# Fetching the V rows of sampled blocks: plain DMAs with register addresses in place of indirect DMAs

## The chip, the cores and the metric

The kernel runs on one core of a Trainium2 chip. A core has a matrix engine (PE), three engines for elementwise work (DVE, ACT and POOL), and SP, whose queue here does nothing but issue DMAs. Each engine runs its own instruction stream in order and waits on semaphores for the others. The metric is device time in microseconds of one execution of the program; lower is better.

## The reference

Block-sparse attention, whose output feeds a feed-forward network with a softplus between its two products. Cut to what is computed:

```python
# q, k, v: (B=4, H=8, S=768, D=64); 24 blocks of 32 rows; sampled_blocks: (24, 3), shared by batches and heads
scores = q @ k.transpose / sqrt(D)
mask = |block_i - block_j| <= 1              # window
mask |= block_i or block_j is 0 or 23        # global rows and columns
mask[block qb, block kb] = True for kb in sampled_blocks[qb]
attn = softmax(where(mask, scores, -1e9))
x = (attn @ v) as (B*S = 3072, H*D = 512)
h = x @ w_in                                 # 512 -> 2048
g = max(h, 0) + log1p(exp(-|h|))
out = g @ w_out                              # 2048 -> 512
```

For most blocks of queries the keys and values that matter are eight blocks of 32: three of the window, blocks 0 and 23, and three sampled ones. Which blocks are sampled is known only at run time.

## The kernel before

**Units of attention.** The blocks of query rows are taken in 24 groups: 4 batches with 6 groups of four blocks (the last group of a batch has two). They stand in `order`. For each batch one more set is added (`whole`), for the rows of blocks 0 and 23, which attend to everything: 28 sets in `sets`. A set is worked in two units of two head pairs each. For a unit, `scores` multiplies queries (tile qc) with gathered keys (tile kg) on PE (L834 for a full group), DVE adds the mask and takes the maximum (L840), `exponents` runs on ACT (L890), `transposes` turns the probabilities on PE (L903) with copies by ACT and DVE (L908, L910), and `values` multiplies them with V rows (tile vg) on PE (L946: 32 instructions in a unit of a full group). `normalise` and `turn` (L975, L989) make the rows of x from that. `pieces` interleaves these: the scores run two units ahead of the values.

**Values in SBUF.** Two buffers, `vbuf[0]` and `vbuf[1]`, serve the sets in turn. In half 0 of a buffer stand the three window blocks of each of the four query blocks (96 partitions); in half 1 stand the three sampled blocks of each (96 partitions); the last 32 partitions of both halves hold blocks 0 and 23. `load_values(m + 2)` is called when the values of set m are issued, and its DMAs wait until PE has read the buffer. For a full group the window rows are one DMA of SP (L755, 96x4x512). The rows of blocks 0 and 23 stay in the buffer for a whole batch. They are loaded with a batch's first two groups (L767), for sets 0 and 1 as 32x512 (L764), which ACT copies three times (`spread_ends`, L737). A whole set fills the buffer with all of the batch's V rows (L748).

**Sampled rows before.** They are fetched by POOL with an indirect DMA for each query block (L773, 96 rows of 2 KB, 88 in all). Its row addresses stand in the tile ix, which `make_index` computes at the start: POOL writes iotas (io, L559), DVE casts them, multiplies the block numbers by 32, adds (L593, three instructions) and adds the start of each batch (L598, four). One more indirect DMA (L564) loads, at the very start, the first rows of V into set 0's buffer, with its own iota (first, L561). The issues are put in the list `value_work`; `attend` takes one from it, and one from `key_work`, at each step (`gather`), and `values` takes what is left of its set first.

**Sampled keys.** These come by POOL's copies from kT, the keys of a batch in SBUF (L715). Their addresses come from registers: `pack_blocks` packs the three block numbers of a query block in 15 bits, two query blocks in a word of the tile pk. `registers` loads such a word into a register of an engine once (L656, TENSOR_LOAD), and shifts and masks take a number from it. The copies of set 0 are on DVE and ACT.

**The rest.** The FFN (L268 to L497) follows behind the attention, mixed into it from about 120 us on. The weights are brought from 64-bit floats by a chain of ACT (L166, L170), DVE (L176, L183, L189, L207) and POOL (L193), one tick for each step of the attention; each weight tile is loaded by SP ten ticks before its conversion begins (L159, tile raw).

**What sets the order.** SP runs in the order of the code. POOL and DVE do so for the startup pieces, and with ACT in the second phase of the FFN; elsewhere a scheduler orders PE, ACT, DVE and POOL by its own model, so that a change in what one instruction waits for can move others. The two places of SP in the loop: `load_values(m + 2)`, `load_queries` (tile qc, L649) and the weight loads (L159) follow each other. SP's DMAs use eight completion semaphores in turn.

Of the kernel before, what the change touches and what calls it, by code (L numbers as in the profile page):

```python
# [8 lines left out]
F32 = mybir.dt.float32  # L9
F32R = mybir.dt.float32r  # L10
I32 = mybir.dt.int32
# [46 lines left out]
def sparse_attention_ffn(  # L58
# [482 lines left out]
    io = ac.tile([NR * BLOCK, 1], I32, name="io")  # L541
    first = ac.tile([P, 1], I32, name="first")
    iof = ac.tile([NR * BLOCK, 1], F32, name="iof")
    ixf = ac.tile([NR * BLOCK, NB], F32, name="ixf")
    ix = ac.tile([NR * BLOCK, B, NB], I32, name="ix")
# [8 lines left out]
    for i in range(NI):  # L554
        nc.gpsimd.iota(
            iu[i * BLOCK : (i + 1) * BLOCK], pattern=[[NI, NG]], base=1 + i, channel_multiplier=0
        )
    for s in range(NR):
        nc.gpsimd.iota(io[s * BLOCK : (s + 1) * BLOCK], pattern=[[0, 1]], base=0, channel_multiplier=1)  # L559
    for rows in (slice(0, NR * BLOCK), slice(NR * BLOCK, P)):  # L560
        nc.gpsimd.iota(first[rows], pattern=[[0, 1]], base=0, channel_multiplier=1)  # L561
    vbuf = [ac.tile([P, 2, NI, DM], F32, name=f"vg{n}") for n in range(2)]

    nc.gpsimd.indirect_dma_start(  # L564
        out=vbuf[0][:, 0, 0, :], out_offset=None, in_=v,
        in_offset=bass.IndirectOffsetOnAxis(ap=first, axis=0),
    )
    nc.vector.memset(mask, 0.0)
    nc.vector.memset(rp, 0.0)

# [13 lines left out]
        )  # L584
        nc.vector.tensor_copy(out=pk, in_=pkf[:, 1 : NB - 1])

    def make_index():
        nc.vector.tensor_copy(out=iof, in_=io)
        nc.vector.tensor_copy(out=rf, in_=blk.rearrange("p (i s w) -> p i s w", s=NR, w=2)[:, :, :, 0])

        for s in range(NR):
            rows = slice(s * BLOCK, (s + 1) * BLOCK)
            nc.vector.tensor_scalar(  # L593
                out=ixf[rows], in0=rf[rows, :, s], scalar1=float(BLOCK), scalar2=iof[rows, 0:1],
                op0=ALU.mult, op1=ALU.add,
            )
        for b in range(B):
            nc.vector.tensor_scalar_add(out=ix[:, b], in0=ixf, scalar1=float(b * S))  # L598

    def make_mask():  # L600
        nc.vector.tensor_copy(out=iuf, in_=iu)
# [65 lines left out]
    def gathered(work, m):  # L667
        while work and work[0][0] <= m:
            work.pop(0)[1]()

    wanted = []

# [16 lines left out]
    def gather_keys(m):  # L689
        b, g = order[m]  # L690
        ni = NI if g < NG - 1 else 2
        kd = kg[m % 2]

        def of_block(i):

            eng = (nc.vector if i < 2 else nc.scalar) if m == 0 else nc.gpsimd
            copy = nc.scalar.copy if m == 0 and i >= 2 else eng.tensor_copy
            if i == 0:
                at = kT[b][:, 4 * g : 4 * g + NR, :]
                pattern = [list(x) for x in at.ap]  # L700
# [8 lines left out]
            (r,) = registers(eng, [2 * g + i // 2])  # L709
            for s in range(NR):  # L710
                x = nc.s_assert_within(
                    eng.snap((r >> (16 * (i % 2) + 5 * s)) & 31), 0, LAST,
                    skip_runtime_bounds_check_because="a sampled block is one of the key blocks",
                )
                copy(  # L715
                    out=kd[:, i, 1 + NR + s, :], in_=kT[b][:, bass.ds(x, 1), :].rearrange("p n f -> p (n f)")
                )
# [21 lines left out]
    def load_values(m):  # L739
# [4 lines left out]
        if whole:  # L744
# [6 lines left out]
            return  # L751
        ni = NI if g < NG - 1 else 2

        i0 = 1 if m == 0 else 0
        nc.sync.dma_start(  # L755
            out=vd[0 : 3 * BLOCK, 0, i0:ni], in_=overlapping(v, b * S + (4 * g + i0) * BLOCK, ni - i0, 3 * BLOCK)
        )
        if g < 2:

            for c, lo in enumerate((b * S, (b + 1) * S - BLOCK)):  # L760
                i1 = i0 if c == 0 else 0
                if m < SPREAD:
                    if i1 == 0:
                        nc.sync.dma_start(out=vd[3 * BLOCK : P, c, 0], in_=v[lo : lo + BLOCK])  # L764
                    spread.append((vd[3 * BLOCK : P, c, 0:1], vd[3 * BLOCK : P, c, 1:]))
                    continue
                nc.sync.dma_start(  # L767
                    out=vd[3 * BLOCK : P, c, i1:],
                    in_=v[lo : lo + BLOCK].unsqueeze(1).to_broadcast([BLOCK, NI - i1, DM]),
                )  # L770

        def of_block(i):
            nc.gpsimd.indirect_dma_start(  # L773
                out=vd[0 : 3 * BLOCK, 1, i, :],
                out_offset=None,
                in_=v,
                in_offset=bass.IndirectOffsetOnAxis(ap=ix[:, b, 4 * g + 1 + i : 4 * g + 2 + i], axis=0),
            )

        value_work.extend((m, lambda i=i: of_block(i)) for i in range(ni))  # L780


    def folded(g, whole):
# [7 lines left out]
    def scores(n):  # L791
# [4 lines left out]
        nmax = st["nmax"] = wk.tile([P, 2, 2], F32, tag="nmax", name=f"nmax{n}", bufs=4)  # L796
        st["pr"] = [wk.tile([P, S], F32, tag="pr", name=f"pr{n}_{r}", bufs=4) for r in range(2)]
        if not whole and g == NG - 1:
            gathered(key_work, place[b, g])
# [19 lines left out]
            st["rows"] = P  # L819
            st["chunks"] = 2  # L820
        elif not whole:
            gathered(key_work, place[b, g])
            kd = kg[place[b, g] % 2]
            ni = NI
            rows = slice(0, ni * BLOCK)
# [187 lines left out]
    def pieces(n):  # L1013
# [7 lines left out]
        def score_piece():  # L1021
# [3 lines left out]
            if s < len(units):  # L1025
                scores(s)
                if scored is not None:
                    load_keys(scored + 2)
                m, a = units[s]
                b, g, whole = sets[m]  # L1030
                if whole and a == NA - 1 and b + 1 < B:

                    gathered(key_work, place[b, g])
                    for n_ in range(4):
                        load_kT(b + 1, n_)
                    load_keys()
# [39 lines left out]
    for n in range(WARM):  # L1076
        nc.tensor.matmul(warm[:, n % 4], ident, ident, start=True, stop=True)
    with tc.manual_schedule(engines={mybir.EngineType.DVE}):
        make_index()
        pack_blocks()  # L1080
        make_mask()
        load_keys(0)
        gathered(key_work, 0)
# [157 lines left out]
```

## Time and profile before

| | |
|---|---|
| time, median of 3 runs | 805.5 us (804.5, 805.5, 806.07) |
| the profiled execution's own time | 807.66 us |
| its span (first to last instruction) | 805.6 us |
| mean granted clock of PE | 0.979 |
| busy PE / DVE / ACT / POOL | 95% / 74% / 70% / 49% |
| indirect DMAs of sampled rows on POOL | 88, 87.9 us |
| bytes moved by DMA | 132.27 MB, 17.57 MB of it in POOL's queue |

The 2.1 us between the span and the time of that execution lie before the first and behind the last instruction. A busy share is a mean over startup, attention with weights being converted, attention with FFN, and FFN alone; the prediction looks at these stages apart.

### The profile page before, as it was taken

The page shows a single profiled execution, that of the slowest core. Times are in us where ns is not written, and L with a number is a line of the kernel's source. Part 1 is how long each engine was busy: PE and PEld are TensorE (multiplying, and loading weights), DVE is VectorE, ACT ScalarE, POOL GpSimd, SP SyncE. Part 2 cuts the span into 40 slices and gives each one's busy share as a digit, 9 for nine tenths or more (in the row PEclk, how much of TensorE's full clock was granted, in tenths as well). Part 3 has the DMA queues.
Part 4 walks back from the last instruction along what each step waited for, and adds up shares of the span by engine and source line. Part 5 has one row for each costly group of instructions (what it writes and reads, how often), then busy time and mean ns, then how long its engine had stood idle before and what let it go on. Part 6 is the DMA issues. An engine that isn't in the chain of part 4 may idle for free.

```text
span 805.6 us, 21589 instructions
## 1 busy us (share of the span) xinstructions
PE 767.6 (95%) x8188; PEld 622.6 (77%) x8188; DVE 597.4 (74%) x1292; ACT 563.4 (70%) x1235; POOL 397.2 (49%) x617
## 2 busy tenths in 40 slices
PE   8688889999899999999999999999999999999997
PEld 8456657777677778777788878888998888988785
DVE  5667898887777777777655657888688797886654
ACT  4767877877687777777665767677776767766552
POOL 6663695543456426455100005425489597695400
PEclk9779998999999999999999999999999999999999
DMA  8669898678697786965714686221302315020021
GB/s 246 214 186 309 256 228 268 189 252 269 183 260 223 242 274 209 256 200 161 246 43 154 218 265 212 68 96 48 105 27 80 104 39 172 12 78 16 27 79 52
DMA packets 61175, 132.27 MB, mean 164 GB/s; under 512 B 5712, under 2 KB 18128, under 8 KB 60048
## 3 DMA queue, kind: packets, MB, share of 16 engines
q1 hardware_dynamic: 55072, 112.41, 44.6%
q0 software_dynamic: 5712, 17.57, 7.6%
q8 instruction: 64, 1.05, 0.6%
q10 hardware_dynamic: 288, 0.93, 0.3%
q14 instruction: 39, 0.32, 0.1%
HBM read 100.47 MB, written 30.41 MB: 162 GB/s over the span
## 4 chain that ended last, share of the span: by engine, by line
PE 55%; DVE 14%; ACT 14%; POOL 8%; issue 4%; DMA 2%; another core or an unknown queue 1%; POOLq 1%; SPq 0%; DVEq 0%; ACTq 0%
PE h L268 8%; PE h L269 7%; PE h L270 7%; PE o L495 5%; ACT pr L890 5%; PE o L496 5%; PE o L497 5%; PE t L903 3%; PE x L946 3%; POOL gq L337 3%; PE s L834 3%; DVE e L285 3%; POOL y L471 2%; PE acc L442 2%; PE acc L441 2%
## 5 line engine op out<-in xcount | busy, mean ns | idle before, releaser
L285 DVE SCALAR_TENSOR_TENSOR e<-u,e 128x512 f32<-128x512 f32 (+1 forms) x108 | 86.1, 797 | 94.4 <-ACT u L283 90.3
L337 POOL TENSOR_TENSOR gq<-gq 128x128 f32<-128x128 f32 x160 | 110.8, 715 | 63.1 <-DVE gq L322 60.0
L890 ACT ACTIVATE pr<-pr,nmax 128x256 f32<-128x256 f32 (+1 forms) x192 | 102.2, 534 | 33.1 <-DVE nmax L840 16.4
L773 POOL DMA_INDIRECT vg<-in_v_dram,ix x88 | 87.9, 998 | 69.8 <-PE x L946 38.3
L294 ACT ACTIVATE u<-u 128x512 f32<-128x512 f32 (+1 forms) x108 | 63.1, 584 | 71.7 <-DVE e L285 70.0
L715 POOL COPY kg<-kT 128x128 f32 x252 | 84.6, 380 | 52.0 <-PE s L834 43.2
L272 ACT ACTIVATE e<-h 128x512 f32<-128x512 f32 (+1 forms) x108 | 59.0, 547 | 57.5 <-PE h L270 57.1
L268 PE MATMUL h<-x,w 128*128 128x512 f32 x240 | 95.7, 399 | 2.4 <-ACT gh L275 1.0
L270 PE MATMUL h<-x,w 128*128 128x512 f32 x240 | 94.6, 394 | 0.0
L269 PE MATMUL h<-x,w 128*128 128x512 f32 x240 | 94.6, 394 | 0.0
L193 POOL TENSOR_TENSOR wt<-wt,raw 128x512 int32<-128x512 int32 x32 | 43.1, 1348 | 70.1 <-ACT raw L170 48.2
L283 ACT ACTIVATE u<-e 128x512 f32<-128x512 f32 (+1 forms) x108 | 63.1, 585 | 17.7 <-DVE gl L359 14.2
L840 DVE CUSTOM_DVE_ANT_1 pr<-s,mask 128x256 f32<-128x256 f32 x160 | 58.1, 417 | 23.3 <-PE s L834 10.4
L268 PE MATMUL h<-x,w1all 128*128 128x384 f32 x192 | 69.1, 360 | 3.4 <-DVE e L289 2.5
L903 PE MATMUL t<-ident,pr 128*128 128x128 f32 x448 | 65.6, 288 | 6.3 <-DVE x L1008 2.4
L270 PE MATMUL h<-x,w1all 128*128 128x384 f32 x192 | 65.2, 340 | 0.0
L269 PE MATMUL h<-x,w1all 128*128 128x384 f32 x192 | 65.2, 340 | 0.0
L277 ACT ACTIVATE e<-e 128x512 f32<-128x512 f32 (+1 forms) x108 | 63.0, 584 | 1.8
L903 PEld LDWEIGHTS t<-ident,pr 128*128 128x128 f32 x448 | 51.3, 145 | 14.1 <-issue 2.8
L946 PEld LDWEIGHTS x<-vg,pt 128*32 128x32 f32 x2560 | 42.8, 114 | 24.0 <-issue 22.4
L495 PE MATMUL o<-w1all,gh 128*128 128x512 f32 x144 | 61.3, 426 | 0.0
L946 PE MATMUL x<-vg,pt 128*32 128x64 f32 x2560 | 53.1, 228 | 7.6 <-issue 7.5
(141 smaller groups left out, 2049.4 us busy)
## 6 DMA issues: line engine op xcount, KB each, us to landing
vg<-in_v_dram SPq DMA_DIRECT2D x19, 768.0 KB
xD<-x SPq DMA_DIRECT2D x8, 1536.0 KB
raw<-in_w_in_dram SPq DMA_DIRECT2D x16, 512.0 KB
raw<-in_w_out_dram SPq DMA_DIRECT2D x16, 512.0 KB
qc<-in_q_dram SPq DMA_DIRECT2D x24, 256.0 KB
vg<-in_v_dram SPq DMA_DIRECT2D x12, 512.0 KB
yD<-os SPq DMA_DIRECT2D x24, 256.0 KB
x<-xD SPq DMA_DIRECT2D x4, 1536.0 KB
```

The source lines that it names most:

```text
L268: nc.tensor.matmul(ph, wh[:, cols], hi[:, c], start=(c == 0), stop=False)
L269: nc.tensor.matmul(ph, wh[:, cols], lo[:, c], start=False, stop=False)
L270: nc.tensor.matmul(ph, wl[:, cols], hi[:, c], start=False, stop=(c == NC - 1))
L283: nc.scalar.activation(u, e, AF.Copy, bias=1.0)
L285: nc.vector.scalar_tensor_tensor(out=e, in0=u, scalar=-1.0, in1=e, op0=ALU.add, op1=ALU.subtract)
L337: nc.gpsimd.tensor_tensor(out=a[:, to], in0=a[:, x], in1=a[:, y], op=op)
L495: nc.tensor.matmul(po[m], gh[:, cols], wh, start=first, stop=False)
L715: copy(out=kd[:, i, 1 + NR + s, :], in_=kT[b][:, bass.ds(x, 1), :].rearrange("p n f -> p (n f)"))
L773: nc.gpsimd.indirect_dma_start(out=vd[0 : 3 * BLOCK, 1, i, :], out_offset=None, in_=v, in_offset=bass.IndirectOffsetOnAxis(ap=ix[:, b, 4 * ...
L890: nc.scalar.activation(x, x, AF.Exp, bias=nmax[rows, r, j : j + 1], scale=-1.0, accum_out=rs[rows, h : h + 1])
L903: nc.tensor.transpose(ps[:, i, 0:rows], st["pr"][r][0:rows, c * P : (c + 1) * P], ident[0:rows, 0:rows])
L946: nc.tensor.matmul(xq[rows, h * D : (h + 1) * D], pt[r, 2 * j + c][:, rows], vd[:, c, i, h * D : (h + 1) * D], start=(c == 0), stop=(c == 1),)
```

## The change

The sampled rows of V are no longer fetched by POOL. `load_values` issues them on SP, directly behind the window rows: for each query block and each of its three sampled blocks one DMA of 32 rows of 512 numbers (64 KB), with the address from a register. There are 12 for a full group and 6 for the last of a batch, 264 in all. The register words are loaded by SP once, eleven in all. `make_index`, its tiles, the iotas and the indirect DMA of the first rows go; of `make_index` only the cast of the block numbers stays (`read_blocks`). Set 0 loads its window rows of all four blocks and the rows of both blocks 0 and 23 by plain DMAs. `value_work` is gone, so `gather` and `gathered` know the keys alone and `values` issues nothing first.

```diff
-    def make_index():
-        nc.vector.tensor_copy(out=iof, in_=io)
+    def read_blocks():
         nc.vector.tensor_copy(out=rf, in_=blk.rearrange("p (i s w) -> p i s w", s=NR, w=2)[:, :, :, 0])
-        for s in range(NR):
-            rows = slice(s * BLOCK, (s + 1) * BLOCK)
-            nc.vector.tensor_scalar(
-                out=ixf[rows], in0=rf[rows, :, s], scalar1=float(BLOCK), scalar2=iof[rows, 0:1],
-                op0=ALU.mult, op1=ALU.add,
-            )
-        for b in range(B):
-            nc.vector.tensor_scalar_add(out=ix[:, b], in0=ixf, scalar1=float(b * S))
...
-    key_work, value_work = [], []
+    key_work = []
     def gather():
-        for work in (value_work, key_work):
-            if work:
-                work.pop(0)[1]()
+        if key_work:
+            key_work.pop(0)[1]()
...
+    def sampled(eng, g, i, s):
+        (r,) = registers(eng, [2 * g + i // 2])
+        return nc.s_assert_within(
+            eng.snap((r >> (16 * (i % 2) + 5 * s)) & 31), 0, LAST,
+            skip_runtime_bounds_check_because="a sampled block is one of the key blocks",
+        )
...
-        i0 = 1 if m == 0 else 0
         nc.sync.dma_start(
-            out=vd[0 : 3 * BLOCK, 0, i0:ni], in_=overlapping(v, b * S + (4 * g + i0) * BLOCK, ni - i0, 3 * BLOCK)
+            out=vd[0 : 3 * BLOCK, 0, 0:ni], in_=overlapping(v, b * S + 4 * g * BLOCK, ni, 3 * BLOCK)
         )
...
-        def of_block(i):
-            nc.gpsimd.indirect_dma_start(
-                out=vd[0 : 3 * BLOCK, 1, i, :],
-                out_offset=None,
-                in_=v,
-                in_offset=bass.IndirectOffsetOnAxis(ap=ix[:, b, 4 * g + 1 + i : 4 * g + 2 + i], axis=0),
-            )
-        value_work.extend((m, lambda i=i: of_block(i)) for i in range(ni))
+        for i in range(ni):
+            for s in range(NR):
+                x = sampled(nc.sync, g, i, s)
+                nc.sync.dma_start(
+                    out=vd[s * BLOCK : (s + 1) * BLOCK, 1, i, :], in_=v[bass.ds(x * BLOCK + b * S, BLOCK)]
+                )
...
-        gathered(value_work, m)
         vd = vg[sets[m]]
...
-        make_index()
+        read_blocks()
         pack_blocks()
...
     with tc.manual_schedule(engines={mybir.EngineType.Pool}):
-        gathered(value_work, 0)
-        gathered(key_work, 1)
+        gathered(1)
```

In the changed kernel the lines of the scores are L808, of the values L919, of the key copies L695, of the window rows L734 and of the sampled rows L752.

Three places show what moves. First SP, at the loads of set 2 (the buffer that set 0 has left; vg is the buffer, qc_3 the queries of order place 3, raw the next weight tiles). Before:

```order
L755 DMA vg_174<-in_v_dram 96x4x512
L649 DMA qc_3_622<-in_q_dram 128x512
L159 DMA raw_662<-in_w_in_dram 128x512
L159 DMA raw_811<-in_w_out_dram 128x512
L755 DMA vg_175<-in_v_dram 96x4x512
```

and of the change the head of that stretch:

```order
L734 DMA vg_164<-in_v_dram 96x4x512
L633 TENSOR_LOAD pk
L633 ISA x2
L752 REGISTER_ALU
L752 ISA
L752 DMA vg_164<-in_v_dram 32x512
L752 REGISTER_ALU x2
L752 ISA
L752 DMA vg_164<-in_v_dram 32x512
```

and its end:

```order
L752 DMA vg_164<-in_v_dram 32x512
L626 DMA qc_3_686<-in_q_dram 128x512
L159 DMA raw_724<-in_w_in_dram 128x512
L159 DMA raw_871<-in_w_out_dram 128x512
L734 DMA vg_165<-in_v_dram 96x4x512
```

Between the window rows and the queries now stand twelve DMAs with their register steps, and a second TENSOR_LOAD after six of them; the queries, the weight tiles and the next set's window rows wait behind them.

Second POOL at the start, from its last iotas to the first key copy of set 1 (kg_180, later kg_169). Before:

```order
L561 IOTA first 96x1
L561 IOTA first 32x1
L564 DMA vg_174<-in_v_dram,first 128x512
L773 DMA vg_174<-in_v_dram,ix 96x512 x4
L656 TENSOR_LOAD pk
L656 ISA x2
L715 REGISTER_ALU
L715 ISA
L715 COPY kg_180<-kT_190 128x128
```

and now:

```order
L550 IOTA iu 32x6 x3
L633 TENSOR_LOAD pk
L633 ISA x2
L695 REGISTER_ALU
L695 ISA
L695 COPY kg_169<-kT_179 128x128
```

The five indirect DMAs ahead of the key copies are gone, and so are the iotas for them.

Third PE, where the scores of set 2 (s, from qc_2) and the values of set 1's first unit (x, from its V buffer) meet; y is the turning of set 0's rows, t the transposes of a unit. Before, the rows around the end of these scores:

```order
L834 MATMUL s_0_668<-kg_179,qc_2_418 32x256
L834 MATMUL s_1_669<-kg_179,qc_2_418 32x256
L989 MATMUL y_710<-ident,xs_640 128x128 x4
L946 MATMUL x_716<-vg_175,pt_0_645 32x64 x8
L946 MATMUL x_716<-vg_175,pt_4_652 32x64 x8
L946 MATMUL x_716<-vg_175,pt_0_645 32x64 x8
L946 MATMUL x_716<-vg_175,pt_4_652 32x64 x8
```

and now, from the transposes to the first of the scores:

```order
L877 MATMUL t_0_707<-ident,pr_0_485 128x128 x2
L877 MATMUL t_4_714<-ident,pr_1_486 128x128 x4
L919 MATMUL x_777<-vg_165,pt_0_708 32x64 x8
L919 MATMUL x_777<-vg_165,pt_4_715 32x64 x8
L919 MATMUL x_777<-vg_165,pt_0_708 32x64 x5
L808 MATMUL s_0_730<-kg_168,qc_2_456 32x256
L808 MATMUL s_1_731<-kg_168,qc_2_456 32x256
```

All 32 instructions of the values stood behind the scores; now 21 of them stand ahead and 11 behind. The following sets show the same with 21 to 25 of 32. The counts of instructions on PE and ACT are about the same as before.

More of the change, by code (lines that the diff above doesn't have):

```diff
@@ L540, in sparse_attention_ffn @@
     pk32 = pk.bitcast(I32)
[L541 to L545, printed above, removed]
     mask = ac.tile([P, NG, NS], F32, name="mask")
@@ L557, in sparse_attention_ffn @@
         )
-    for s in range(NR):
-        nc.gpsimd.iota(io[s * BLOCK : (s + 1) * BLOCK], pattern=[[0, 1]], base=0, channel_multiplier=1)
-    for rows in (slice(0, NR * BLOCK), slice(NR * BLOCK, P)):
-        nc.gpsimd.iota(first[rows], pattern=[[0, 1]], base=0, channel_multiplier=1)
     vbuf = [ac.tile([P, 2, NI, DM], F32, name=f"vg{n}") for n in range(2)]
-    nc.gpsimd.indirect_dma_start(
-        out=vbuf[0][:, 0, 0, :], out_offset=None, in_=v,
-        in_offset=bass.IndirectOffsetOnAxis(ap=first, axis=0),
-    )
     nc.vector.memset(mask, 0.0)
@@ L585, in pack_blocks @@
         nc.vector.tensor_copy(out=pk, in_=pkf[:, 1 : NB - 1])
-    def make_index():
-        nc.vector.tensor_copy(out=iof, in_=io)
+    def read_blocks():
         nc.vector.tensor_copy(out=rf, in_=blk.rearrange("p (i s w) -> p i s w", s=NR, w=2)[:, :, :, 0])
-        for s in range(NR):
-            rows = slice(s * BLOCK, (s + 1) * BLOCK)
-            nc.vector.tensor_scalar(
-                out=ixf[rows], in0=rf[rows, :, s], scalar1=float(BLOCK), scalar2=iof[rows, 0:1],
-                op0=ALU.mult, op1=ALU.add,
-            )
-        for b in range(B):
-            nc.vector.tensor_scalar_add(out=ix[:, b], in0=ixf, scalar1=float(b * S))
     def make_mask():
@@ L657, in registers, with gathered @@
         return [regs[eng, u] for u in us]
-    key_work, value_work = [], []
+    key_work = []
     def gather():
-        for work in (value_work, key_work):
-            if work:
-                work.pop(0)[1]()
-    def gathered(work, m):
-        while work and work[0][0] <= m:
-            work.pop(0)[1]()
+        if key_work:
+            key_work.pop(0)[1]()
+    def gathered(m):
+        while key_work and key_work[0][0] <= m:
+            key_work.pop(0)[1]()
+    def sampled(eng, g, i, s):
[4 more added lines that the diff above has]
+        )
     wanted = []
@@ L708, in of_block @@
                 end_keys(m, (first, nc.scalar.copy))
-            (r,) = registers(eng, [2 * g + i // 2])
+            registers(eng, [2 * g + i // 2])
             for s in range(NR):
[L711 to L714, printed above, removed]
+                x = sampled(eng, g, i, s)
                 copy(
@@ L760, in load_values @@
             for c, lo in enumerate((b * S, (b + 1) * S - BLOCK)):
-                i1 = i0 if c == 0 else 0
                 if m < SPREAD:
-                    if i1 == 0:
-                        nc.sync.dma_start(out=vd[3 * BLOCK : P, c, 0], in_=v[lo : lo + BLOCK])
+                    nc.sync.dma_start(out=vd[3 * BLOCK : P, c, 0], in_=v[lo : lo + BLOCK])
                     spread.append((vd[3 * BLOCK : P, c, 0:1], vd[3 * BLOCK : P, c, 1:]))
@@ L767, in load_values @@
                 nc.sync.dma_start(
-                    out=vd[3 * BLOCK : P, c, i1:],
-                    in_=v[lo : lo + BLOCK].unsqueeze(1).to_broadcast([BLOCK, NI - i1, DM]),
-                )
-        def of_block(i):
-            nc.gpsimd.indirect_dma_start(
-                out=vd[0 : 3 * BLOCK, 1, i, :],
-                out_offset=None,
-                in_=v,
-                in_offset=bass.IndirectOffsetOnAxis(ap=ix[:, b, 4 * g + 1 + i : 4 * g + 2 + i], axis=0),
-            )
-        value_work.extend((m, lambda i=i: of_block(i)) for i in range(ni))
+                    out=vd[3 * BLOCK : P, c],
+                    in_=v[lo : lo + BLOCK].unsqueeze(1).to_broadcast([BLOCK, NI, DM]),
+                )
+        for i in range(ni):
[4 more added lines that the diff above has]
+                )
     def folded(g, whole):
@@ L798, in scores @@
         if not whole and g == NG - 1:
-            gathered(key_work, place[b, g])
+            gathered(place[b, g])
             kd = kg[place[b, g] % 2]
@@ L821, in scores @@
         elif not whole:
-            gathered(key_work, place[b, g])
+            gathered(place[b, g])
             kd = kg[place[b, g] % 2]
@@ L1031, in score_piece @@
                 if whole and a == NA - 1 and b + 1 < B:
-                    gathered(key_work, place[b, g])
+                    gathered(place[b, g])
                     for n_ in range(4):
@@ L1082, in sparse_attention_ffn @@
         load_keys(0)
-        gathered(key_work, 0)
+        gathered(0)
     load_queries(1)
```

## The prediction

> **What bounds the kernel now.** I read the busy shares first, then the same shares by stage, because a mean over 800 us hides stages with different limits.
>
> ```profile
> PE 767.6 (95%) x8188; PEld 622.6 (77%) x8188; DVE 597.4 (74%) x1292; ACT 563.4 (70%) x1235; POOL 397.2 (49%) x617
> ...
> 0.00:120.00 120.00, 100.02 (x1610) 72.75 (x1614) 88.57 (x271) 85.18 (x214) 80.06 (x149) 0.91 0.82 240
> 120.00:425.00 305.00, 294.94 (x4493) 228.84 (x4493) 231.36 (x634) 226.49 (x584) 137.97 (x241) 0.98 0.72 217
> 425.00:806.00 381.00, 372.65 (x2095) 321.02 (x2093) 277.50 (x389) 251.72 (x437) 179.14 (x228) 1.00 0.29 98
> ...
> 100.00:120.00 20.00, 16.38 (x249) 11.76 (x247) 20.00 (x43) 16.13 (x43) 19.27 (x29) 1.00 0.90 228
> ```
>
> In the rows of windows the numbers after the length are the busy us of PE, PEld, DVE, ACT and POOL, then the granted clock, the DMA share and GB/s. From 120 us on PE is busy for 294.94 of 305 and 372.65 of 381 us: 18.4 us without a matmul in 686. The change takes no matmul away, so nothing much can be won there. In the first 120 us PE lacks 20 us. That is where this change can pay, and where it can hurt, since the DMA engines are 0.82 busy there. Around 100 to 120 us the bound is not PE: DVE has no idle time at all (20.00 of 20) and POOL hardly any (19.27).
>
> The waits of PE come next.
>
> ```profile
> PE x L946 <- issue: 7.5, 16, 1.1
> PE s L834 <- POOL kg L715: 3.2, 1, 3.2
> PE t L903 <- DVE x L1008: 2.4, 1, 2.4
> ```
>
> (Total us, times, longest.) No matmul of `values` (tile x, L946) waits for its V rows: its only wait is "issue". The indirect loads are in time today, so nothing is won by having sampled values sooner. What the change can win must come from POOL and DVE.
>
> **What leaves POOL.** The sampled loads are one group of the page:
>
> ```profile
> L773 POOL DMA_INDIRECT vg<-in_v_dram,ix x88 | 87.9, 998 | 69.8 <-PE x L946 38.3
> ```
>
> 88 issues of 998 ns, 87.9 us of POOL's 397.2. From 120 us on I take their value as nothing, because PE hides them: POOL is at 137.97 of 305 there. The largest thing that could be exposed behind POOL is the 2.4 us wait of L903 above; that is the upper end, and zero the lower. I take zero, since POOL is less than half busy.
>
> Before 120 us it differs. The rows of DVE and POOL around 115 us, with one L189 in a quiet place first:
>
> ```profile
> 34.39 0.74 DVE L189 SCALAR_TENSOR_TENSOR wt<-raw,wt 128x512 int32<-128x512 int32 x1
> ...
> 115.82 1.17 POOL L773 DMA_INDIRECT vg<-in_v_dram,ix  x1 [0.17 <-PE o L497]
> 117.01 1.29 POOL L193 TENSOR_TENSOR wt<-wt,raw 128x512 int32<-128x512 int32 x1
> 118.47 1.19 POOL L773 DMA_INDIRECT vg<-in_v_dram,ix  x1 [0.16 <-issue]
> 119.68 1.31 POOL L193 TENSOR_TENSOR wt<-wt,raw 128x512 int32<-128x512 int32 x1
> ...
> 116.57 2.30 DVE L189 SCALAR_TENSOR_TENSOR wt<-raw,wt 128x512 int32<-128x512 int32 x1
> 119.39 2.02 DVE L359 TENSOR_TENSOR gl<-u,gh 128x384 fp32r<-128x384 f32 x1
> 121.94 0.54 DVE L359 TENSOR_TENSOR gl<-u,gh 128x384 fp32r<-128x384 f32 x1
> ```
>
> L189 takes 0.74 us alone and 2.30 us here. It begins during the indirect, and ends 0.57 us after the L193 behind it. L359 does the same at 119.39: 2.02 us instead of 0.54, from inside the second indirect to after the second L193. I read this as DVE being held first by the indirect and then, POOL's next instruction being ready at once, by L193. Without the indirects both DVE instructions could finish in their usual time: (2.30 - 0.74) + (2.02 - 0.54) = 3.04 us. Both stand on the chain that ended last:
>
> ```profile
> 116.57 2.30 DVE wt L189
> ...
> 119.47 1.94 DVE gl L359
> ```
>
> So **3.0 us** is the gain that I can point to. Its lower end is nothing (L193 stays and can meet the same instructions elsewhere).
>
> The Trainium skill, "SBUF — State Buffer", section "Who interferes with whom", speaks against this gain. It says that a DVE instruction with two SBUF inputs collides with a GpSimd instruction that reads SBUF but not with one that only writes it, and infers that making DMA descriptors needs the write side alone. By that rule only L193 held these two and the 3.0 us stay, giving 805.5; the trace speaks rather against it, as L189 began 0.44 us before L193 and should have kept its place.
>
> **The start.** `make_index` loses eight DVE instructions (about 0.2 us each, ahead of the packing of the block numbers) and POOL eight indirects. The warm-up matmuls hide them:
>
> ```profile
> 1.45 14.35 PE L1077 MATMUL warm<-ident 128*128 128x128 f32 x100 [1.45 <-POOL ident masks.py:199]
> 15.73 2.18 PE L834 MATMUL s<-kg,qc 64*32 64x256 f32 x64
> ...
> 23.90 2.49 PE L834 MATMUL s<-kg,qc 64*32 64x256 f32 x32 [3.19 <-POOL kg L715]
> ...
> 12.43 4.38 POOL L715 COPY kg<-kT 128x128 f32 x12
> ```
>
> The first scores follow the warm-up directly. The scores of set 1 at 23.90 are put down to POOL's key copies, but these ended at 16.8, seven us earlier: they aren't what was late, and ending them sooner is worth nothing. I take 0, with 3.2 us (the whole idle time) as the other end.
>
> **What SP gets.** Twelve loads of 32 rows for each whole set, 264 in all. The same shape of DMA, the register loads, and the register steps as POOL does them for its key copies:
>
> ```profile
> L764 SPq DMA_DIRECT2D vg<-in_v_dram x3: 321/322/696, 2.7 to 10.4; - x3
> L656 POOLq TENSOR_LOAD <-pk x11: 5/286/502, 8.3 to 22.2; - x11
> 202.14 4.30 POOL L715 COPY kg<-kT 128x128 f32 x18
> ```
>
> (min/median/max ns.) One issue is 0.322 us; 18 copies with their register steps take 4.30 us, so the steps cost at most 0.239 us: 0.56 us a load, between 0.32 and, with the slowest issue in the rows below, 1.02. In all 264 x 0.56 = 148 us on a queue that now stands waiting for V buffers alone for 113.4:
>
> ```profile
> SPq L755 <- PE x L946: 113.4, 15, 13.5
> ...
> 33.05 0.34 SPq L755 DMA_DIRECT2D vg<-in_v_dram  x1
> 33.43 1.02 SPq L649 DMA_DIRECT2D qc<-in_q_dram  x1
> 34.49 0.43 SPq L159 DMA_DIRECT2D raw<-in_w_in_dram  x1
> 34.97 0.43 SPq L159 DMA_DIRECT2D raw<-in_w_out_dram  x1
> ...
> 36.14 0.99 PE L946 MATMUL x<-vg,pt 128*32 128x64 f32 x33
> 42.87 1.10 PE L946 MATMUL x<-vg,pt 128*32 128x64 f32 x64
> 47.68 0.87 PE L946 MATMUL x<-vg,pt 128*32 128x64 f32 x47
> ...
> 54.94 1.96 PE L834 MATMUL s<-kg,qc 64*32 64x256 f32 x32
> ...
> 23.29 1.47 SPq L159 DMA_DIRECT2D raw<-in_w_in_dram  x3
> ...
> 31.70 0.69 ACT L166 ACTIVATE wt<-raw 128x512 f32<-128x512 f32 x1
> 55.58 0.68 ACT L166 ACTIVATE wt<-raw 128x512 f32<-128x512 f32 x1
> ...
> 0.77 5.59 DMA blk<-in_blocks_dram
> ```
>
> Set 2 is the tight place. Its buffer comes free at 33.05 and its values are wanted at 47.68. A landing is taken as 5.59 us, the row of the block table. SP's DMAs take eight completion semaphores in turn, so an issue also waits for the landing of the one eight before it: 5.59 / 8 = 0.70 us a load, more than the 0.56. Twelve loads are issued by 33.05 + 0.34 + 12 x 0.70 = 41.8 and the last lands at **47.4**: just in time. Behind them on SP stand the queries of order place 3 and two weight loads, 8.4 us later than now. The queries move from 33.4 to 41.8 and are wanted at 54.94. The first of the two weight loads goes from 34.5 to 43 and is the fourth to be converted, at 55.58. So both are covered, by 7 us after the landing; without that cover up to 8.4 us would stand open, which the late rival holds.
>
> Sets 0 and 1 share one run of SP that begins when the block numbers are packed (8.3 us, the first register load). Set 0's twelve land at 8.3 + 0.3 + 8.4 + 5.6 = 22.6, and its values follow the scores of 23.90. Three window and end loads, another register load and set 1's twelve end at 17.0 + 0.3 + 15 x 0.70 = 27.8 and land at 33.4, wanted at 36.14. The first three weight loads follow at 28.2 instead of 23.29 and land by 34; the first conversion is at 31.70 now, but ACT's new order puts it behind the exponentials of the unit in front of it (2 us), so about 33.7. This too is just in time. Later sets have more room, as values take longer with FFN matmuls between them.
>
> **What PE gets.** The order of instructions on PE changes as well. At five places before about 86 us, 21 to 25 of the 32 instructions of `values` stand ahead of the next scores instead of behind them. All 32 are 64 matmuls of 1.10 us (42.87), so the scores start up to 25/32 x 1.10 = 0.86 us later, near 0.72 at the fewest; and the values are done as much earlier. I take nothing, because the sum of PE's work is the same; 5 x 0.72 = 3.6 us is the other end, and a gain of that size is as conceivable.
>
> **The sum.** The profiled execution took 807.66 us with a span of 805.6. 807.66 - 3.0 = 804.7; that execution is 2.2 us over the median 805.5, so the forecast is 805.5 - 3.0 = **802.5 us**.
>
> **Rivals.**
>
> **No change, 805.5 us.** The change does move the work, but PE hides all of it: DVE is held by L193 alone, or the weights that come sooner out of DVE wait for PE. For it: 95% PE. Against: L189 begins before L193.
>
> **Scores late, 809.1 us.** 3.6 us from PE's new order on 805.5. It decides if the start of scores ends the chain between 30 and 86 us, that is if ACT and DVE stand idle until those scores. For it: ACT's exponentials stand on the chain there, and PE waits in this stretch. Against: the values come earlier by the same amount. With the 3.0 us gained beside it the result would be 806.1, no change.
>
> **Sampled rows late, 813 us.** SP issues serially what POOL gathered in one piece. With 1.02 us a load, set 2 lands at 33.05 + 0.34 + 12.2 + 5.6 = 51.2, 3.5 us after 47.68. Three such sets (2, 3, 4, before FFN matmuls widen the gaps) give 10.6 us: 802.5 + 10.6 = 813. It decides at a landing above 5.7 us, which is 0.1 us from the row that I used; the DMA engines are 0.82 busy there. Against: that row is from the start, when all large loads are in flight.
>
> The Trainium skill, "DMA: Bandwidth & Descriptors", section "Rules for kernel authors", says to coalesce many small transfers and that under 64 KB one pays mostly overhead; these are 64 KB each. Its "Anatomy of one DMA" fits about 2.0 us + bytes / 436e3 (a fit for GpSimd's path), as an estimate 2.15 us each: 25.8 us for twelve in series, which would miss 47.68 by far, and 0.27 us each with eight in flight, which would not. No run here shows which.
>
> **How the numbers follow.** Forecast 0.40; no change 0.20; scores late 0.15; sampled rows late 0.25, as three places are in time by less than 3 us. The forecast's own range is 797 to 804: 802.5 less 3.2 (start) and 2.4 (L903) is 796.9, and half of the 3.0 lost is 804. The range of all reaches over no change and 809.1 to 813, and leaves out the worse half of the late rows. A measurement of this kernel can tell 0.2%, about 1.6 us: faster 0.40, within 0.20, slower 0.15 + 0.25 = 0.40.
>
> **What would show it.** Right: no L189 or L359 of 2 us between 100 and 125 us, DVE below 20.00 of 20 there, and no wait of L919 (the new line of values) for `vg`. Wrong: a wait of values for SP's loads in sets 0 to 4; a step of SP over 0.7 us a load; queries or weights that PE, ACT or DVE wait for; a start of scores that moved by more than 0.8 us with DVE idle before it. If DVE's holds are gone and the time is the same, the stretch was not on the path.

## The result and the profile after

The changed kernel takes **853.16 us** (median of 4 runs, 852.02 to 857.4) beside 805.67 us before: a ratio of 1.0602, 95% interval 1.0563 to 1.064. The forecast was 802.5 us, the range ended at 813: the sign was wrong.

The busy shares and the same three stages as before, the last one longer (columns: length, busy us of PE, PEld, DVE, ACT, POOL, clock, DMA share, GB/s):

```profile
PE 789.0 (93%) x8188; PEld 628.0 (74%) x8188; DVE 593.9 (70%) x1284; ACT 565.3 (66%) x1235; POOL 317.2 (37%) x523
...
0.00:120.00 120.00, 95.92 (x1552) 71.23 (x1553) 81.67 (x254) 80.36 (x201) 46.82 (x108) 0.90 0.74 215
120.00:425.00 305.00, 276.24 (x3910) 203.03 (x3911) 206.08 (x549) 202.05 (x519) 89.26 (x186) 0.98 0.72 207
425.00:851.00 426.00, 416.83 (x2728) 353.77 (x2727) 306.15 (x483) 282.92 (x516) 181.10 (x231) 1.00 0.30 102
```

POOL has lost its 80 us as planned. The span is 45.2 us longer (850.8 after 805.6 us), in two parts of about the same size. The time in which no matmul runs grows from 38.0 to 61.8 us. And PE's busy time grows too, from 767.6 to 789.0 us, for the same 8188 matmuls. (Busy is the time in which at least one matmul runs; matmuls overlap, and the profile models their ends.)

Between 120 and 425 us, where PE was busy for 294.94 of 305 us with 4493 matmuls, it is now busy for 276.24 with 3910. A stage in which "nothing can be won" had much to lose. The waits of PE (total, times, longest) name two new kinds:

```profile
PE o L495 <- ACT gh L347: 17.1, 13, 2.0
PE t L877 <- DVE nmax L814: 7.6, 13, 1.6
...
PE x L919 <- DMA vg<-in_v_dram: 3.7, 3, 2.3
```

PE stands at the projections of the FFN (tile o), waiting for ACT, and at the transposes, waiting for DVE. For the sampled rows themselves it waits only 3.7 us. SP's timeline around set 2 and the chain of waits there:

```profile
33.87 0.34 SPq L734 DMA_DIRECT2D vg<-in_v_dram  x1
35.13 13.34 SPq L752 DMA_DIRECT2D vg<-in_v_dram  x12
48.52 0.41 SPq L626 DMA_DIRECT2D qc<-in_q_dram  x1
...
33.87 11.13 DMA vg<-in_v_dram
...
48.52 2.83 DMA qc<-in_q_dram
51.49 1.96 PE s L808 x32
...
L752 SPq DMA_DIRECT2D vg<-in_v_dram x264: 315/316/1628, 8.5 to 463.8; - x132
...
DMA to landing us min/median/max: 1.7/3.5/11.7
```

An issue costs the 0.316 us that were expected, but twelve hold SP for 13.34 us, 1.11 us each. The window load ahead of them takes 11.13 us to land, the sampled loads queue behind it, and with eight of its DMAs in flight SP has to wait. Only then come the queries, at 48.52, and the scores start when they have landed.

PE's timeline at one later place shows the new order at work (the first row is the last of a run of eighteen projections that begins at 243.90):

```profile
247.95 0.39 PE L496 MATMUL o<-w1all,gh 128*128 128x512 f32 x1
248.27 0.32 PE L919 MATMUL x<-vg,pt 128*32 128x64 f32 x8
249.50 0.73 PE L497 MATMUL o<-w1all,gl 128*128 128x512 f32 x2 [0.91 <-DVE gl L359]
...
252.64 0.40 PE L497 MATMUL o<-w1all,gl 128*128 128x512 f32 x1
252.96 0.86 PE L919 MATMUL x<-vg,pt 128*32 128x64 f32 x42
253.75 1.09 PE L808 MATMUL s<-kg,qc 64*32 64x256 f32 x32
...
255.14 0.42 PE L919 MATMUL x<-vg,pt 128*32 128x64 f32 x14
```

Projections stand between a unit's values, and the next scores behind all of them. The 64 matmuls of the unit come in three pieces.

### The profile page after: what moved, and what is told of

Its sections match the earlier page's. It is cut to its first block, busy times and chain, and to the rows that moved or that the text cites. A ratio compares the mean times of both kernels' runs of the same rounds, so it can differ in the third digit from the quotient of the medians.

```text
span 850.8 us, 22839 instructions
## 1 busy us (share of the span) xinstructions
PE 789.0 (93%) x8188; PEld 628.0 (74%) x8188; DVE 593.9 (70%) x1284; ACT 565.3 (66%) x1235; POOL 317.2 (37%) x523
## 4 chain that ended last, share of the span: by engine, by line
PE 52%; DVE 15%; ACT 12%; DMA 8%; POOL 7%; issue 3%; SPq 2%; POOLq 0%; DVEq 0%; ACTq 0%
PE h L268 7%; PE h L270 7%; PE h L269 7%; DMA vg<-in_v_dram 5%; PE o L495 5%; PE o L497 5%; PE o L496 5%; ACT pr L864 3%; PE s L808 3%; POOL gq L337 3%; PE x L919 3%; DVE e L285 2%; POOL y L471 2%; DVE pr L814 2%; PE t L877 2%
## 5 line engine op out<-in xcount | busy, mean ns | idle before, releaser
L285 DVE SCALAR_TENSOR_TENSOR e<-u,e 128x512 f32<-128x512 f32 (+1 forms) x108 | 84.2, 780 | 89.8 <-ACT u L283 89.5
L695 POOL COPY kg<-kT 128x128 f32 x252 | 90.2, 404 | 131.4 <-PE s L808 111.4
L193 POOL TENSOR_TENSOR wt<-wt,raw 128x512 int32<-128x512 int32 x32 | 46.1, 1441 | 156.8 <-ACT raw L170 58.6
L919 PEld LDWEIGHTS x<-vg,pt 128*32 128x32 f32 x2560 | 47.6, 115 | 41.2 <-issue 26.8
L919 PE MATMUL x<-vg,pt 128*32 128x64 f32 x2560 | 64.2, 231 | 9.0 <-DMA vg<-in_v_dram 3.7
L497 PE MATMUL o<-w1all,gl 128*128 128x512 f32 x144 | 59.6, 422 | 3.8 <-DVE gl L359 3.8
```

The source lines that it names most:

```text
L285: nc.vector.scalar_tensor_tensor(out=e, in0=u, scalar=-1.0, in1=e, op0=ALU.add, op1=ALU.subtract)
L497: nc.tensor.matmul(po[m], gl[:, cols], wh, start=False, stop=last)
L695: copy(out=kd[:, i, 1 + NR + s, :], in_=kT[b][:, bass.ds(x, 1), :].rearrange("p n f -> p (n f)"))
L919: nc.tensor.matmul(xq[rows, h * D : (h + 1) * D], pt[r, 2 * j + c][:, rows], vd[:, c, i, h * D : (h + 1) * D], start=(c == 0), stop=(c == 1),)
```

## The experiments

Two theories: **SP**, that its queue holds back what stands behind the loads; and **PE's order**, that the scheduler's new order costs time by itself. To part them, PE is put in the order of the code. One line does it, and then the order on PE is the same whatever SP does:

```diff
-    with _tile.TileContext(nc) as tc, tc.manual_schedule(engines={_mybir.EngineType.SP}):
+    with _tile.TileContext(nc) as tc, tc.manual_schedule(engines={_mybir.EngineType.SP, _mybir.EngineType.PE}):
```

All ratios are to the kernel before, run on the same chip beside them (it took 804.6, 804.0, 793.4 and 793.3 us beside r1 to r4, r5 to r8, r9 to r12 and r13 to r15, so times of different groups aren't compared). Why the kernel before is 11 us faster in the last two groups isn't known; its granted clock is 0.979 to 0.988 in the first two and 0.987 to 0.995 in the last two. Ratios of the first two groups are therefore not compared with those of the last two to better than some 1.4%.

| run | ratio | 95% interval |
|---|---|---|
| the change | 1.0602 | 1.0563 to 1.064 |
| r1 before, PE in code order | 1.0068 | 1.0045 to 1.0091 |
| r2 the change, PE in code order | 1.0305 | 1.0261 to 1.035 |
| r3 r1 with dummy loads on SP | 1.0329 | 1.0274 to 1.0385 |
| r4 r2, one load a query block | 0.9884 | 0.9863 to 0.9906 |
| r5 r2, queries first | 1.0097 | 1.0064 to 1.013 |
| r6 r2, window behind | 1.0338 | 1.0267 to 1.0408 |
| r7 r2, loads spread | 1.0046 | 1.0017 to 1.0075 |
| r8 queries first, PE scheduled | 1.0817 | 1.0779 to 1.0855 |
| r9 r4 with free indirects | 1.0941 | 1.0909 to 1.0972 |
| r10 r4, PE scheduled | 0.9927 | 0.9896 to 0.9958 |
| r11 r7, PE in code order in the first phase | 1.0124 | 1.0093 to 1.0155 |
| r12 before, the same | 1.0033 | 1.0012 to 1.0055 |
| r13 r4 with gated indirects | 1.0577 | 1.0548 to 1.0606 |
| r14 r4 with gated copies on POOL | 1.0139 | 1.0112 to 1.0166 |
| r15 indirects in batch 0, then spread | 0.9963 | 0.9941 to 0.9985 |

**PE's order against SP: r1 to r4.**

r1 and r2 are the one line above on both kernels.

> The kernel before, with PE's instructions in the order of the code (nearly the order that it had). All theories: 803 to 809 us. It is the base for the other kernels with PE fixed.

> The changed kernel, with PE's instructions in the order of the code, so the same order on PE as in r1. PE's new order is the cause: 803 to 812 us. SP is the cause (twelve loads of 0.66 us and 4.7 us of waits for completion semaphores hold queries, weights and the next window back): 840 to 860 us, as the changed kernel itself (853). Both share it: between, 820 to 835.

r3, on r1:

```diff
+    dummy = [ac.tile([BLOCK, 16], F32, name=f"dummy{n}") for n in range(NR * NI)]
...
         value_work.extend((m, lambda i=i: of_block(i)) for i in range(ni))
+        if m >= SPREAD:
+            for i in range(NR * ni):
+                nc.sync.dma_start(out=dummy[i], in_=v[i * BLOCK : (i + 1) * BLOCK, 0:16])
```

> r1 with twelve loads of 32 x 64 bytes more on SP behind each window load from set 2 on (into a tile that nobody reads); the indirect DMAs stay on POOL. Time that SP is held is the cause: 825 to 850 us, since only queries, weights and next windows are later here. Sampled rows that land late, or their bytes, are the cause: 803 to 811.

r4, on r2:

```diff
         for i in range(ni):
-            for s in range(NR):
-                x = sampled(nc.sync, g, i, s)
-                nc.sync.dma_start(
-                    out=vd[s * BLOCK : (s + 1) * BLOCK, 1, i, :], in_=v[bass.ds(x * BLOCK + b * S, BLOCK)]
-                )
+            x = sampled(nc.sync, g, i, 0)
+            nc.sync.dma_start(out=vd[0 : 3 * BLOCK, 1, i, :], in_=v[bass.ds(x * BLOCK, 3 * BLOCK)])
```

> r2 with one load of 96 consecutive rows for each query block, from the first sampled number, in place of three of 32 (the other two sampled blocks and the batch's offset are left out). As many bytes, a third of the loads. Count on SP is the cause: 803 to 815 us. Bytes, or that values wait for SP's DMAs at all, is the cause: 840 to 860.

Both theories hold a share. From r2 to the change, with only PE's order set differently (ACT, DVE and POOL stay with the scheduler and follow it), the ratio goes from 1.0305 to 1.0602: some 24 us are PE's order. From r1 to r2, with PE's order the same, it goes from 1.0068 to 1.0305: some 19 us are SP, less what dropping the indirects gains. r3 loses as much by SP's time alone (1.0329), although the rows are still gathered by POOL and hardly a byte is added. r4 moves as many bytes in a third of the loads and is *faster* than before, and than the 803 to 815 us expected, so the bytes are not the matter. It leaves out two of the three sampled blocks and the batch's offset, and so do r9, r10, r13 and r14, which are built on it: they are probes and no kernels to use. Beside r4 (795.37 us), r2 (828.2 us) loses 33 us to its loads on SP.

The two shares look different on PE. The busy times of r1, then r2:

```profile
PE 762.3 (94%) x8188; PEld 617.1 (76%) x8188; DVE 597.6 (74%) x1292; ACT 563.7 (70%) x1235; POOL 396.1 (49%) x617
```

```profile
PE 764.3 (92%) x8188; PEld 623.5 (75%) x8188; DVE 591.3 (72%) x1284; ACT 564.9 (68%) x1235; POOL 309.9 (37%) x523
```

From r1 to r2 PE is busy about as long, and its time without a matmul grows from 45.3 us (of 807.6) to 62.0 (of 826.3): SP's share is waiting. From r2 to the change the time without a matmul stays, 62.0 and 61.8 us, and the busy time grows from 764.3 to 789.0: waits for queries give way to waits for ACT and DVE, and the share of PE's order is the same matmuls overlapping less. The granted clock isn't the reason, as it is higher in the change (0.978 after 0.968). The matmuls of the values show it, before and then in the change:

```profile
L946 PE MATMUL x<-vg,pt 128*32 128x64 f32 x2560 | 53.1, 228 | 7.6 <-issue 7.5
```

```profile
L919 PE MATMUL x<-vg,pt 128*32 128x64 f32 x2560 | 64.2, 231 | 9.0 <-DMA vg<-in_v_dram 3.7
```

One of them takes as long as before (231 and 228 ns), but together they are busy for 64.2 us instead of 53.1. A unit's 64 matmuls in one piece, here in r2, take 1.10 us; the three pieces above take 0.32 + 0.86 + 0.42 = 1.60.

```profile
149.68 1.10 PE L919 MATMUL x<-vg,pt 128*32 128x64 f32 x64
```

PE goes from the matmuls of one kind of tile (h, o, s, t, x, y, acc) to those of another 407 times in r2 and 486 times in the change.

What r2's PE waits for, first in its list:

```profile
PE s L808 <- DMA qc<-in_q_dram: 16.1, 7, 7.9
```

**What stands behind the loads: r5 to r8.** r5 (on r2) and r8 (on the changed kernel) issue the queries first:

```diff
                 values(n)
-                if ended[2] is not None:
-                    load_values(ended[2] + 2)
             if scored is not None:
                 load_queries(scored + 2)
+            if n < len(units) and ended[2] is not None:
+                load_values(ended[2] + 2)
```

> r2 with the queries issued on SP ahead of the next value loads instead of behind them. In r2 PE waits 16.1 us for queries (tile qc). Queries behind the loads are the whole cost of SP: 809 to 814 us. Weight loads, next windows or the sampled rows themselves are as late: 820 to 828.

> The changed kernel with the queries issued ahead of the next value loads, PE left to the scheduler. If the late queries are what made the scheduler collect FFN projections ahead of scores: 812 to 820 us. If its order stays bad for another reason: 835 to 853.

r6, on r2, issues the sampled loads ahead of the window load from set 2 on (`of_blocks` is the loop over i and s):

```diff
+        if m >= SPREAD:
+            of_blocks()
         nc.sync.dma_start(
             out=vd[0 : 3 * BLOCK, 0, 0:ni], in_=overlapping(v, b * S + 4 * g * BLOCK, ni, 3 * BLOCK)
         )
...
+        if m < SPREAD:
+            of_blocks()
```

> r2 with the window rows (and the rows of blocks 0 and 23) issued behind the twelve sampled loads from set 2 on. The waits for completion semaphores that window and weight loads hold (about 4.7 of 12.6 us a set) are a part of the cost: 815 to 823 us. Only the 0.66 us a load counts: 826 to 830, as the same twelve stand before the queries.

r7, on r2, puts the loads of a query block into the list `value_work` again, of which each step takes one entry:

```diff
-        for i in range(ni):
+        def of_block(i):
             for s in range(NR):
                 x = sampled(nc.sync, g, i, s)
...
+        value_work.extend((m, lambda i=i: of_block(i)) for i in range(ni))
```

> r2 with the twelve loads issued in portions of three, one portion at each step of the attention, as the indirect DMAs were, so that queries and weight loads aren't behind all twelve. What stands behind the burst is the cost: 796 to 806 us (POOL without indirects gave 795 in r4). The number of loads on SP is the cost, however they are placed: 820 to 828.

The queries are about half of what SP's loads cost r2 beside r4: r5 is at 1.0097, 2.1% or 17 us under r2, and PE's wait for them (16.1 us) is gone. It is still 2.1% over r4; its values now wait 6.9 us for V rows, and the rest isn't taken apart. r6 refutes a part of my account: with the window behind the sampled loads the ratio stays (1.0338) and PE still waits 16.3 us for queries:

```profile
PE s L814 <- DMA qc<-in_q_dram: 16.3, 5, 5.8
```

So the order of window and sampled loads doesn't matter while both stand ahead of the queries. r7 comes to 1.0046; its 807.53 us lie just over the 796 to 806 expected. And r8 lies outside both of its ranges: with queries first and PE left to the scheduler the kernel is slower than the change itself. From 120 to 425 us, r8 and then r5:

```profile
120.00:425.00 305.00, 275.79 (x3634) 196.38 (x3629) 199.25 (x544) 201.31 (x506) 86.15 (x189) 0.98 0.66 198
...
120.00:425.00 305.00, 292.75 (x4533) 227.21 (x4533) 226.89 (x636) 230.26 (x592) 85.57 (x187) 0.99 0.76 225
```

The same loads in the same order on SP, 3634 matmuls against 4533: here the order on PE, with what follows from it on ACT and DVE, costs 7%. Again most of it is busy time: 806.5 us after 764.5 in r5, with 588 changes from one kind of matmul to another after 407, while the time without a matmul grows from 49.3 to 58.8. Why the scheduler orders so was not tried; its model isn't in these runs.

**Where the gain of r4 comes from, and a kernel that keeps it: r9 to r15.** r10 is r4 with the scheduler's order on PE.

> r4 with PE left to the scheduler, which then gives the order of the kernel before: 786 to 795 us if the loss of the changed kernel is its loads on SP and the order that follows from them; over 800 if the scheduler's order costs time by itself.

At 0.9927 r10 is within its expectation: with few loads on SP, dropping the indirects gains 0.7% (0.4 to 1.0). The scheduler's order adds no busy time then (PE is busy 755.9 us, 755.4 in r4), though it isn't quite that of the kernel before. r4 gained 1.8% on r1. r1 and r4 between 40 and 70 us, and the waits that r1 has and r4 has not:

```profile
40.00:70.00 30.00, 24.32 (x542) 16.53 (x540) 22.02 (x71) 22.18 (x64) 19.62 (x31) 0.94 0.87 258
...
PE x L946 <- issue: 8.0, 14, 1.9
...
PE s L834 <- issue: 3.2, 5, 1.7
```

```profile
40.00:70.00 30.00, 27.36 (x556) 18.66 (x556) 26.97 (x83) 27.25 (x74) 11.26 (x23) 1.00 1.02 319
```

In r1 PE stops again and again inside one group of its matmuls, waiting for nothing that the profile shows, mostly while POOL issues indirects; DVE and ACT then have less to do. In r4 no wait of PE is put down to "issue". But the stalls don't follow from the indirects alone. r12, below, has all 88 of them and r1's order on PE, ACT, DVE and POOL up to the second phase of the FFN; it ran in the third group, and its only such wait is at the scores:

```profile
PE s L834 <- issue: 3.2, 3, 2.4
```

And r2 and r5, which have no indirects, have one stop of 2.1 us each at the values. What brings these stalls is open, and with it how much of r4's gain belongs to the indirects.

r9 and r13 were to put the issue of indirects back into r4 without their bytes, r14 POOL's time without a DMA. r9 (88 indirects of 96 rows of 64 bytes into tiles that nobody reads) and, behind the dots, the two lines that differ in r13 (80 indirects of 32 rows of 64 bytes into the last rows of the V buffer, which they overwrite):

```diff
+            nc.gpsimd.indirect_dma_start(
+                out=dummy[i], out_offset=None, in_=v.rearrange("a (n c) -> (a n) c", c=16),
+                in_offset=bass.IndirectOffsetOnAxis(ap=first, axis=0),
+            )
...
+                out=vd[3 * BLOCK : P, 1, i, 0:16], out_offset=None, in_=v.rearrange("a (n c) -> (a n) c", c=16),
+                in_offset=bass.IndirectOffsetOnAxis(ap=first[0:BLOCK], axis=0),
```

> r4 with the 88 indirect DMAs back on POOL at their old steps, but each of 96 rows of 64 bytes into a tile that nobody reads. In r1 PE has 22 stalls of over 0.15 us inside groups of its own instructions while an indirect runs (11.8 us), in r4 none; r1 and r4 differ by 14 us. That POOL issues indirect DMAs is what stalls PE: 803 to 810 us, with the stalls back. Their bytes, or the V rows coming sooner, are what counts: 794 to 798, without stalls.

> r9 was confounded: nothing held its indirects back, so they stood in bursts of 4 to 20 ahead of POOL's key copies and PE waited 31.9 us for keys. Here each small indirect (32 rows of 64 bytes, from set 2 on) writes into rows of the V buffer that it serves (they overwrite a part of the last block's rows), so it waits for the buffer as the indirects of before did. The issue of indirects on POOL is what costs the 14 us between r4 and r1: ratio to before 1.000 to 1.007. The 192 KB that each of them moved in POOL's queue, or the DVE holds that end with them, are the cost: 0.985 to 0.992.

r14, in r13's place for each indirect:

```diff
+            nc.gpsimd.tensor_copy(out=vd[3 * BLOCK : P, 1, i, :], in_=vd[3 * BLOCK : P, 1, i, :])
```

> r13 with a copy on POOL (32x512, onto itself) in place of each indirect: POOL's time is spent, no DMA. POOL's time is the cost: 1.000 to 1.007. It is not: 0.985 to 0.992.

r9 and r13 don't answer the question; each made a wait of its own that neither r1 nor r4 has. r9, then r13:

```profile
PE s L819 <- POOL kg L699: 31.9, 4, 14.9
```

```profile
PE x L932 <- DMA vg<-in_v_dram,first: 30.1, 19, 5.4
```

r9's indirects waited for nothing and stood in front of the key copies; r13's were put late and the values waited for them. The stalls of r1 came back in neither (1.2 and 0.2 us of "issue" in all). r14 has no such wait of its own. At 1.0139 it lies over both of its ranges, and 2.6% over r4 (0.9884):

```profile
L757 POOL COPY vg<-vg 32x512 f32<-32x512 f32 x80 | 59.0, 776 | 37.7 <-PE x L926 36.7
```

That is 59.0 us of POOL, which points to POOL's time not being free at these steps. But r4 ran in the first group and r14 in the fourth, and a copy is no indirect, so it isn't a price, and it doesn't tell how the gain splits between POOL's time and PE's stalls. That stays open.

r11 and r12 give the later FFN phase back to the scheduler (the line in the program's context goes):

```diff
+    in_code = ctx.enter_context(ExitStack())
+    in_code.enter_context(tc.manual_schedule(engines={mybir.EngineType.PE}))
...
         if j == SECOND:
+            in_code.close()
```

> r7 (loads spread over the steps) with PE in the order of the code only until the second phase of the FFN, where the scheduler takes over. r1 ended its attention 5 us before the kernel before and lost 9 later, so the scheduler's second phase should give back 4 to 9 us: 799 to 804 us. If the late phase isn't where r1 lost: 806 to 809.

> The kernel before with the same half fixed order, the control for r11: 799 to 805 us by r1's times; the same as r1 (809) if the late phase isn't where r1 lost.

r12 lies at 1.0033, a little under r1. r11 is at 1.0124, over r7 (1.0046) where 4 to 9 us less were expected. In us it is 6 under r7 (801.44 after 807.53) and in its range; the ratio is larger because the kernel before is 11 us faster in r11's group. Which of the two comparisons holds isn't known. What r7 loses to r4 (the same order on PE, and nearly the same time of the kernel before beside them) it has lost by about 100 us: the first scores of the second batch begin at 102.35 us against 90.24, and no later group of scores or values is more than 13.1 us behind. So r15 keeps the indirects for the first batch and lets SP fetch the rest in portions:

```diff
-        value_work.extend((m, lambda i=i: of_block(i)) for i in range(ni))
+        def of_blocks(i):
+            for s in range(NR):
+                x = sampled(nc.sync, g, i, s)
+                nc.sync.dma_start(
+                    out=vd[s * BLOCK : (s + 1) * BLOCK, 1, i, :], in_=v[bass.ds(x * BLOCK + b * S, BLOCK)]
+                )
+        value_work.extend((m, lambda i=i: of_blocks(i) if b else of_block(i)) for i in range(ni))
```

> r12 with the sampled rows of the first batch by indirect DMAs as before, those of the other three by SP in portions of three a step as in r11. SP's loads cost nothing once FFN matmuls stand between the sets (after about 120 us), and the indirects cost some 5 to 8 us there: ratio 0.990 to 0.997, better than before and than r11 (1.012). SP's loads cost as much in every batch: 1.005 to 1.012.

**0.9963 (0.9941 to 0.9985)**: faster than both kernels, by little against the kernel before, and 0.7% under its control r12. Its rows from 120 us on, under r12's:

```profile
120.00:425.00 305.00, 294.79 (x4497) 230.18 (x4496) 229.14 (x622) 225.97 (x580) 136.96 (x239) 0.99 0.69 211
```

```profile
120.00:425.00 305.00, 299.86 (x4529) 235.50 (x4528) 225.46 (x625) 228.96 (x585) 79.07 (x179) 1.00 0.75 224
```

With FFN matmuls between the sets, 198 loads on SP cost no more than the 66 indirects that they replace, and PE is busy 5 us more of 305.

## Why the prediction was wrong

- **"I take nothing" for PE's order.** This step failed most. Its bound of 3.6 us was worked out from five places before 86 us, and from values standing ahead of scores. The cost is about 24 us (r2 to the change), nearly all behind 120 us, where projections are gathered ahead of scores and values are cut in pieces. "The sum of PE's work is the same" was the wrong premise: the number of matmuls is the same (8188), but PE is busy 789.0 us with them in the change, after 767.6 before and 764.3 in r2, because they overlap less in the new order.
- **"The queries ... are wanted at 54.94".** A misread row: 54.94 is the second unit of set 3. The first begins at

```profile
44.93 0.62 PE L834 MATMUL s<-kg,qc 64*32 64x256 f32 x5
```

  Against 41.8 + 5.6 = 47.4 the queries were late by 2.5 us on my own figures. I called that covered by 7 us; measured, PE waits 16.1 us for queries in r2, and issuing them first gains 17 us (r5). In the change itself that wait is 0.6 us, as PE has other work put ahead of the scores.
- **0.70 us a load.** 1.11 us at set 2. The landing was taken from a load that ran early (5.59 us); the window load ahead of the twelve took 11.13 us, and SP waited for it. The bare issue was right (0.316 us measured, 0.322 taken).
- **Sampled rows late, the rival at 813 us.** It had the right engine and the wrong victim: values waited for their rows 3.7 us in all, and what came late was the queue's next customer. The Trainium skill, "DMA: Bandwidth & Descriptors", section "Rules for kernel authors" (coalesce small transfers), pointed the right way: a third of the loads with the same bytes took r2's 1.0305 to r4's 0.9884. The estimate of 2.15 us for one load of 64 KB, worked out ahead from the fit in its "Anatomy of one DMA", lies between the shortest and the median landing here, 1.7 and 3.5 us.
- **The gain of 3.0 us.** The holder was misread. In the kernel before, 25 of the instructions L189 and L359 run beside an indirect, and 23 of them take their usual time (0.67 to 0.74 and 0.54 to 0.56 us); only the two quoted, with an L193 behind the indirect, are long. So the indirect alone doesn't hold DVE, as the first rival had it. The rule of the Trainium skill that I set against this gain ("SBUF — State Buffer", section "Who interferes with whom") fits these rows better than I said. The two long holds are gone, and DVE is busy 19.31 of 20 us from 100 to 120:

```profile
100.00:120.00 20.00, 17.67 (x294) 12.79 (x292) 19.31 (x48) 17.71 (x43) 17.72 (x36) 1.00 0.75 189
```

  But L193 still meets L359 elsewhere in the change (1.66 us at 247.79, 288.93 and 389.23; PE's 0.91 us of waiting at 249.50 is for the first), so the 3.0 us aren't shown to be won. With SP relieved the kernel is 0.7 to 1.2% faster than before (r10, r4), 6 to 9 us. A term left out stood in a quoted row: PE's 7.5 us of "issue" in 16 pieces. At the values it is gone in r4 and 0.2 us in r10, but it is gone in r12 as well, with all the indirects, so no run shows it to be their price.
- **The start, at 0.** Scores of set 1 began at 21.08 us instead of 23.90, a gain of 2.8 inside the 0 to 3.2 given. The first scores of set 2 were then late, 36.84 against 33.83.

## What to carry to other kernels

Before work is moved to a queue with much idle time, list what stands behind it there, and find for each the first instruction that wants it; here the queue was free enough for the loads and too slow for the queries behind them. A bound engine's row of "95% busy" says that little can be gained there, not that little can be lost: if a scheduler orders it, compare its order over the whole program, not at the first places that differ. And count how often the engine goes from one kind of matmul to another: the same number of matmuls isn't the same time. Give a transfer's landing time from the place where it will run, behind the large loads that stand ahead of it.

## What the runs showed of the hardware

The same matmuls take PE longer when they alternate with others: 64 matmuls of the values 1.10 us in one piece and 1.60 us in three, all 8188 matmuls 764.3 us of busy time in r2's order and 789.0 in the change's.

PE can stall inside one group of matmuls without a cause that the profile shows: at the values 7.5 us in 16 pieces before and 8.0 us in 14 in r1, both with indirects; none in r4 without them, but also none in r12 with them. The cause is not shown.

An L359 of DVE (two inputs, 128x384) that begins beside POOL's L193 takes up to 1.66 us in the change, where 0.55 is usual. Beside an indirect alone, L189 and L359 took their usual time in all 23 cases before.

Loads behind a window load land in a row right after it, however early they were issued. At set 2 the window rows landed at 45.0 us, the sampled load issued at 35.13 us landed at 45.2 and the one issued at 41.38 at 46.4. Those issued once the window had landed took 1.7 to 1.8 us.
